# A transformer block in one hand-ordered kernel: down weights on SP's queue, and the order dealt anew

## The chip, the cores and the metric

The kernel runs on one core of a Trainium2 chip. A core has five engines with a queue of instructions each: TensorE (PE in the profile; its weight loads are listed as PEld), VectorE (DVE), ScalarE (ACT), GpSimd (POOL) and SyncE (SP), which here only issues transfers. Each takes its instructions in order and waits at semaphores. Transfers are carried by 16 DMA engines that all queues share. The metric is the time of one execution on the device in microseconds (us); the time before is the median of three runs.

## The reference

Input is x with 2048 rows of 1024, in bf16. Attention has 32 heads of 32 for the queries and one head for keys and values; the second half is a gated block with 3584 hidden columns.

```
h  = x + attention(layernorm(x)) @ wo
     q = layernorm(x) @ wq   (32 heads),  k, v = layernorm(x) @ wk, @ wv   (one head)
     p = softmax(q k^T / sqrt(32)),  o = p v
h2 = h + (sigmoid(n @ w_gate) * (n @ w_up)) @ w_down      with n = layernorm(h)
```

## The kernel before, in words

The 2048 rows are 16 tiles of 128; two tiles are a *unit*, so there are eight units. Keys and values of all rows and the queries are made first, then attention and the gated block run interleaved: while one unit is in attention, earlier ones are in the gated block.

**Attention** is cut into 512 *bursts*. A burst is four score matmuls side by side (line 888), which fill two pairs of PSUM banks, and two exponentials of 128 x 1024 on ScalarE (line 908) that read them into bf16 tiles (`Pr`, at first also free parts of `QT` and `wo`). There are three pairs of banks, so burst k waits for the first exponential of burst k-1. The products with V follow in chains of eight steps (line 995), with VectorE adding up the exponentials for the sums (945, 957) and matmuls with ones finishing them (1042, 1057).

**The rest of TensorE's work** goes between bursts, in *steps* of one 512-column matmul (line 382) or of four 32-column matmuls side by side (line 384) that do the same work; eight steps accumulate into one of two PSUM banks. Such groups are the output projection of a tile, gate or up columns of a tile (256 x 2 columns each), and the down projection (28 steps). A gate group is evacuated by ScalarE (tanh, line 1359), an up group by VectorE (1399), which writes `gu`; SP transposes that to `hact` (1383). After the output projection VectorE takes the second layernorm's statistics; GpSimd makes mean and reciprocal deviation (473 to 488), VectorE writes `hn`, and SP transposes it into `QT` (line 633): only then can gate and up of this tile begin.

**Weights.** Gate and up weights come again for every unit in *slabs* of 512 KB (`load_halves`), into whichever buffer is free: `wgu`, used-up parts of `QT`, at the end `Pr`, `kT4` and `zone`. If only a unit's first tile is ready, a slab may be held for the second tile (`may_hold`) or is loaded once more. The down weights stay: 14 loads of 512 KB into `zone` (`load_wd`), as the room of the queries' weights and of the transposed first layernorm comes free.

**What sets the order.** The Python that builds the program keeps a clock for each engine and one for the transfers (`k_dma`). Each instruction adds a written cost to its engine's clock, each transfer or transposition gets a time at which it counts as landed (`dma`, `transposed`), and the main loop chooses what TensorE does next by what counts as ready: the next burst when the exponential it waits for counts as done (`due`), otherwise attention chains by the letters of `PV_PLAN`, or a group. `PV_HOLD` says how long past that moment a chain may go on. Where a long stretch has nothing ready, `fill` puts in matmuls of 128 columns that nobody reads (line 418). So the order is fixed in the program; on the chip the semaphores alone decide when each instruction starts, and a transfer that lands later than it was counted stops the engine at that place, with everything behind it.

In `load_wd` GpSimd waits for the matmuls that last read the room, and for the last 12 loads also for an exponential, so that the load isn't issued early:

```
                need(pool, *ticks)
                if wd_next[0] >= NFP - WD_LATE:
                    need(pool, (c_e, 2 * k[0] - 2))
```

`LN_LEAD` and `LN_RATE` say how many tiles of the first layernorm must be done before some query work, `T_PLAN` and `Q_PLAN` which engine evacuates query tiles, `TODO` the order of the first groups, `U_PLAN` when a unit's output projection is urgent, `TURN` when down loads pause ahead of a transposition, `I_MAX` how many instructions of column-tiled steps may be dense.

Of the kernel before, what the change touches and what calls it, by code (L numbers as in the profile page):

```python
# [12 lines left out]
P = 128  # L13
# [73 lines left out]
def bass_sequential_preLN__grouped_kv_mqa__glu_gated_glu__prompt_kernel(  # L87
# [23 lines left out]
    NFP = NFT // 2  # L111
# [5 lines left out]
    RP = 18  # L117
    HR = 4
    NGU = 4
    U_PLAN = "07293057"  # L120
    PV_PLAN = "EAaabCdaAbadaDdbDAbaCeBDadaadaaaAaaaaAaaDbaBaaaaaadaBBDaaabCaaEdAbDaABDA"
    WO_PLAN = "bbbaabba"
    PV_HOLD = 1.25
    BANK_WAIT = 0
    NPB = 4
    G_SUM, HCH, HB0 = 4, 4, 2
    LN_LEAD = 3
    LN_RATE = 0.25
    T_PLAN = "aaaaddaddaddddad"
    H_ROOM = 0.2  # L130
    Q_PLAN = "ddaaadddddddaddddddddddddddddddd"
    SUM_PLAN = "ppppdddp"
    HOLD0 = 2
    HOLD7 = 2
    D_PLAN = "00000000"
    K_BUSY = 10
    TODO = ["q1b", "q3c", "C1", "q3b", "q1a", "v0", "Q4", "q0d", "q3a", "k1", "k2", "q2b", "C3", "q2a", "v4", "v6",
            "k3", "q1d", "C2", "v3", "v7", "v5", "q1c", "q0c", "v1", "q2c", "q2d", "q3d", "v2"]
# [14 lines left out]
    NU = len(UNITS)  # L153
    UNIT = {t_: c_ for c_, ts_ in enumerate(UNITS) for t_ in ts_}
    LAST_G = [max(g_ for g_, x_ in enumerate(ORDER) if UNIT[x_[0]] == c_) for c_ in range(NU)]
    WD_FROM, WD_GAP, WD_LATE = 10, 3, 12
    WD_GAP2 = 1
    TURN = 0
    LATE = 0.05
    I_BLOCK, I_LAT = 256, 4.5  # L160
    H_GAP = 3
# [1 line left out]
    H_LEAD = 2.0  # L163
    H_OUT = 4
    QREC = 32
    QORD = 0
    URG0 = 0
    K_ACT = 0
    T_MM, T_FIX, T_SW, T_EXP, T_TANH, T_ADD = 0.0004167, 0.00267, 0.0985, 0.9165, 0.479, 0.61

    xf = A_x[0]
# [2 lines left out]
    with ExitStack() as es:  # L174
# [33 lines left out]
        k_pe, k_dve, k_act, k_pool, k_sp, k_dma = [0.0], [0.0], [0.0], [0.0], [0.0], [0.0]  # L208
# [13 lines left out]
        d_wo, d_wd = ctr("d_wo"), ctr("d_wd")  # L222
# [55 lines left out]
        def _(unused):  # L278
            sp, pe, act, dve, pool = nc.sync, nc.tensor, nc.scalar, nc.vector, nc.gpsimd

            def dma(q, dst, src, c, kb=256, rate=285.0, lat=None):
                q.dma_start(dst, src).then_inc(c.sem, 16)
                c.n += 16
                begin = max(CLK[id(q)][0], k_dma[0])
                k_dma[0] = begin + kb / rate
                c.at[c.n] = k_dma[0] + (lat or 1.15 + kb * 0.0037) + (0.8 if q is pool else 0.0)
                return (c, c.n)

# [69 lines left out]
                need(pe, f(True) if callable(f) else f)  # L358
                bank_free[b] = "open"

            main = [False]

            issued = collections.deque()
            part = [0]
            I_US, I_MAX = 4.0, 210

            def by_columns(g):
                if not main[0] or g.items[0][0] < 0.05:
# [261 lines left out]
            def transposed(eng, dst, src, slot, *ticks):  # L630
                need(eng, *ticks)
                c, clk = d_t[slot], CLK[id(eng)]
                eng.dma_start_transpose(dst, src).then_inc(c.sem, 16)
                c.n += 16
                queued = eng is sp and len(x_val) == NT and k_dma[0] > clk[0]
                clk[0] += 1.3
                if eng is sp:
                    k_dma[0] = max(clk[0], k_dma[0]) + 1.2
                c.at[c.n] = max(clk[0], k_dma[0] if eng is sp else 0.0) + (1.9 if queued else 0.7)
                return (c, c.n)  # L640

            k_val, v_val, q_val = {}, {}, {}
# [1063 lines left out]
            def turning():  # L1706
# [175 lines left out]
```

## Time and profile before

| | us |
|---|---|
| median of three runs (1089.45 to 1093.27) | 1090.58 |
| profiled execution | 1090.78 |
| its span | 1089.0 |
| TensorE busy | 1055.4 |
| ScalarE busy | 1008.4 |
| VectorE busy | 900.1 |
| GpSimd busy | 64.5 |

Busy times are of the span. A matmul of 512 columns is listed with some 380 ns, but the next one starts long before its end, so busy TensorE isn't TensorE at its peak; the exponentials on ScalarE overlap in the same way. In the rows by time a bracket such as [0.45 <-PE S_ps L888] is idle time of the engine before the row, and what ended it. In the rows on waits stand the total, the number and the longest. The chain goes back from the last instruction to what released each step; a DMA row in it runs from issue to landing.

### The profile page before, as it was taken

The page shows a single profiled execution, that of the slowest core. Times are in us where ns is not written, and L with a number is a line of the kernel's source. Part 1 is how long each engine was busy: PE and PEld are TensorE (multiplying, and loading weights), DVE is VectorE, ACT ScalarE, POOL GpSimd, SP SyncE. Part 2 cuts the span into 40 slices and gives each one's busy share as a digit, 9 for nine tenths or more (in the row PEclk, how much of TensorE's full clock was granted, in tenths as well). Part 3 has the DMA queues.
Part 4 walks back from the last instruction along what each step waited for, and adds up shares of the span by engine and source line. Part 5 has one row for each costly group of instructions (what it writes and reads, how often), then busy time and mean ns, then how long its engine had stood idle before and what let it go on. Part 6 is the DMA issues. An engine that isn't in the chain of part 4 may idle for free.

```text
span 1089.0 us, 25646 instructions
## 1 busy us (share of the span) xinstructions
PE 1055.4 (97%) x10436; PEld 424.9 (39%) x10537; DVE 900.1 (83%) x1491; ACT 1008.4 (93%) x1152; POOL 64.5 (6%) x136
## 2 busy tenths in 40 slices
PE   8999999999999999999999999999999999999999
PEld 7643333333333333333333333333333333333344
DVE  6889888888988888899988897889888989879621
ACT  6999999999999999999999999999999999999410
POOL 2341111000000000000000000000000000000000
PEclk9999999999999999999999999999999999999999
DMA  7557359953989469982999649990999459990880
GB/s 195 123 120 234 88 129 267 213 122 112 299 203 282 117 160 268 259 196 79 291 247 248 177 106 303 242 250 27 269 296 304 121 152 292 309 298 21 233 236 25
DMA packets 278677, 215.46 MB, mean 198 GB/s; under 512 B 100256, under 2 KB 272544, under 8 KB 278560
## 3 DMA queue, kind: packets, MB, share of 16 engines
q1 hardware_dynamic: 273744, 204.12, 72.5%
q0 software_dynamic: 2592, 9.44, 3.1%
q8 instruction: 83, 1.36, 0.5%
q10 hardware_dynamic: 2224, 0.26, 0.2%
q14 instruction: 34, 0.28, 0.1%
HBM read 187.30 MB, written 4.19 MB: 176 GB/s over the span
## 4 chain that ended last, share of the span: by engine, by line
PE 79%; ACT 8%; DMA 6%; issue 4%; DVE 3%; POOL 1%; SPq 0%; POOLq 0%; ACTq 0%
PE X_ps L382 44%; PE X_ps L384 13%; PE S_ps L888 13%; PE X_ps L995 9%; ACT Pr L908 7%; DMA wgu<-in_B_w_up_dram 2%; DMA QT<-hn 1%; DMA wgu<-in_B_w_gate_dram 1%; DMA zone<-in_A_wv_dram 1%; ACT wo L908 1%; DMA QT<-in_B_w_up_dram 1%; PE X_ps L1042 1%; DVE pairs L945 1%; POOL sd L484 0%; PE X_ps L1057 0%
## 5 line engine op out<-in xcount | busy, mean ns | idle before, releaser
L908 ACT ACTIVATE Pr<-S_ps 128x1024 bf16<-128x1024 f32 x992 | 933.8, 1066 | 6.7 <-PE S_ps L888 6.0
L945 DVE TENSOR_TENSOR pairs<-Pr 128x1024 bf16<-128x1024 bf16 x470 | 320.6, 684 | 30.5 <-ACT Pr L908 29.7
L957 DVE TENSOR_TENSOR pairs<-pairs 128x1024 bf16<-128x1024 bf16 x408 | 281.6, 690 | 12.1
L888 PE MATMUL S_ps<-QT,kT 32*128 32x512 bf16 x2048 | 202.0, 385 | 4.7 <-ACT wo L908 1.1
L382 PE MATMUL X_ps<-wgu,QT 128*128 128x512 bf16 x777 | 198.0, 380 | 7.2 <-issue 3.7
L382 PE MATMUL X_ps<-zone,hact 128*128 128x512 bf16 (+2 forms) x675 | 156.4, 371 | 4.0 <-issue 3.5
L888 PEld LDWEIGHTS S_ps<-QT,kT 32*128 32x128 bf16 x2048 | 51.5, 91 | 211.3 <-ACT Pr L908 198.1
L382 PE MATMUL X_ps<-QT 128*128 128x512 bf16 x480 | 124.0, 380 | 5.2 <-issue 2.2
L995 PE MATMUL X_ps<-Pr,V 128*32 128x512 bf16 x1984 | 126.9, 381 | 0.6 <-ACT Pr L908 0.6
L1399 DVE SCALAR_TENSOR_TENSOR gu<-gu,X_ps 128x512 bf16<-128x512 f32 x112 | 76.6, 684 | 44.8 <-PE X_ps L382 38.1
L382 PEld LDWEIGHTS X_ps<-wgu,QT 128*128 128x128 bf16 x817 | 71.5, 98 | 99.2 <-issue 22.2
L1359 ACT ACTIVATE gu<-X_ps 128x512 f32<-128x512 f32 x112 | 71.3, 636 | 36.2 <-PE X_ps L382 36.2
L382 PEld LDWEIGHTS X_ps<-zone,hact 128*128 128x128 bf16 x705 | 60.9, 98 | 78.2 <-issue 19.3
L995 PEld LDWEIGHTS X_ps<-Pr,V 128*32 128x32 bf16 x1984 | 46.6, 96 | 57.1 <-issue 14.1
L382 PEld LDWEIGHTS X_ps<-QT 128*128 128x128 bf16 x504 | 44.3, 98 | 61.6 <-issue 12.7
L382 PE MATMUL X_ps<-wo,QT 128*128 128x512 bf16 x232 | 58.1, 380 | 0.9 <-issue 0.5
L473 POOL CAST mean<-mv 128x1 f32<-128x1 bf16 x28 | 6.6, 235 | 864.3 <-DVE mv L1210 832.4
L384 PE MATMUL X_ps<-zone,hact 128*32 128x512 bf16 x876 | 55.4, 380 | 0.0
L382 PE MATMUL X_ps<-zone 128*128 128x128 bf16 (+3 forms) x548 | 49.5, 238 | 2.5 <-DVE QT L772 0.8
L384 PE MATMUL X_ps<-wgu,QT 128*32 128x512 bf16 x748 | 51.1, 381 | 0.4 <-DVE ols L1087 0.2
L384 PE MATMUL X_ps<-QT 128*32 128x512 bf16 x688 | 46.4, 380 | 1.3 <-DVE olp L1011 0.6
L1435 DVE SCALAR_TENSOR_TENSOR hx<-X_ps,hx 128x512 bf16<-128x512 f32 (+2 forms) x33 | 22.2, 672 | 24.4 <-PE X_ps L382 22.6
(116 smaller groups left out, 612.8 us busy)
## 6 DMA issues: line engine op xcount, KB each, us to landing
wgu<-in_B_w_up_dram SPq DMA_DIRECT2D x90, 512.0 KB, 6.1
wgu<-in_B_w_gate_dram SPq DMA_DIRECT2D x87, 512.0 KB, 6.0
QT<-in_B_w_gate_dram SPq DMA_DIRECT2D x65, 512.0 KB, 6.3
QT<-in_B_w_up_dram SPq DMA_DIRECT2D x64, 512.0 KB, 6.2
zone<-in_B_w_down_dram POOLq DMA_DIRECT2D x14, 512.0 KB, 4.8
hx<-in_A_x_dram SPq DMA_DIRECT2D x17, 256.0 KB, 2.8
out_dram<-hx SPq DMA_DIRECT2D x31, 128.0 KB, 1.7
Pr<-in_B_w_gate_dram SPq DMA_DIRECT2D x5, 512.0 KB, 6.4
```

The lines of the kernel that those rows point to most:

```text
L382: return pe.matmul(out, lhsT=lhsT, rhs=rhs, start=start, stop=stop, skip_group_check=main[0])
L384: ins = pe.matmul(out[DH * j:DH * (j + 1)], lhsT=lhsT[:, DH * j:DH * (j + 1)], rhs=rhs, start=start, stop=stop, tile_position=(0, DH * j), ...
L473: return c_pool.inc(pool.tensor_copy(out=mean[:, i:i + 1], in_=mv[:, i:i + 1, 0]), 0.2)
L888: ins = pe.matmul(S_ps[:, ((2 * k + j // 2) % 3) * 2 + j % 2, :], lhsT=kT4[DH * j:DH * (j + 1), kt * P:(kt + 1) * P], rhs=rows(t)[DH * j:D ...
L908: c_e.inc(act.activation(out=p_tile(k, n % 2), in_=S_ps[:, 2 * pr:2 * pr + 2, :].rearrange("p a (b q) -> p (a b) q", q=QC), func=ACTF.Exp, ...
L945: slot_use[x] = c_dve.inc(dve.tensor_tensor(out=dst(x), in0=p_tile(k - 1, hh), in1=p_tile(k, hh), op=ALU.add), T_ADD, 0.08)
L957: slot_use[x] = slot_use[y] = c_dve.inc(dve.tensor_tensor(out=pairs[:, x, :], in0=pairs[:, x, :], in1=pairs[:, y, :], op=ALU.add), T_ADD, ...
L995: ins = pe.matmul(bank[DH * j:DH * (j + 1), :], lhsT=V[:, kt, :], rhs=p_tile(kx, j // 2)[:, j % 2 * 2:j % 2 * 2 + 2, :], start=b == bs[0], ...
L1042: ins = pe.matmul(bank[DH * j:DH * (j + 1), :], lhsT=ones[:], rhs=pairs[:, sum_wide[(g, j // 2)], j % 2 * 512:(j % 2 + 1) * 512], start=Tr ...
L1359: tanh_val[n] = c_act.inc(act.activation(out=slot, in_=bank, func=ACTF.Tanh, scale=0.5), T_TANH, 0.1)
L1399: v = c_dve.inc(dve.scalar_tensor_tensor(out=slot.bitcast(BF16)[:, 0:512], in0=slot, scalar=1.0, in1=bank, op0=ALU.add, op1=ALU.mult), 0.6 ...
L1435: v = c_dve.inc(dve.scalar_tensor_tensor(out=hv, in0=bank[:, 0:n], scalar=0.5, in1=hv, op0=ALU.mult, op1=ALU.add), 0.03 + n * 0.00113, 0.08)
```

## The change

The 14 loads of down weights go to SP's queue, where the slabs and the transpositions are issued, and are counted there as slabs are; GpSimd's waits for exponentials fall away, and with them the use of `WD_LATE`. A transposition that is queued behind other transfers counts as landing 3.1 us after its turn instead of 1.9, another one in the main loop 1.5 instead of 0.7. GpSimd's remaining transfers count as slower. `PV_HOLD` falls from 1.25 to 0.5, `BANK_WAIT` and the other numbers change as shown, and with new costs and plans the order of the whole program is dealt anew. No work of the reference is added or removed; the number of gate and up slabs falls from 320 to 304, the fillers of line 418 rise from 89 to 154.

```
-    U_PLAN = "07293057"
+    U_PLAN = "75761920"
...
-    PV_HOLD = 1.25
-    BANK_WAIT = 0
+    PV_HOLD = 0.5
+    BANK_WAIT = 0.3
...
-    LN_LEAD = 3
-    LN_RATE = 0.25
-    T_PLAN = "aaaaddaddaddddad"
+    LN_LEAD = 1
+    LN_RATE = 0.35
+    T_PLAN = "aaaaaddddddaadaa"
...
-    WD_FROM, WD_GAP, WD_LATE = 10, 3, 12
+    WD_FROM, WD_GAP, WD_LATE = 10, 3, 14
     WD_GAP2 = 1
-    TURN = 0
+    TURN = 1
...
-    QORD = 0
-    URG0 = 0
-    K_ACT = 0
+    QORD = 1
+    URG0 = 1
+    K_ACT = 1
...
                 begin = max(CLK[id(q)][0], k_dma[0])
-                k_dma[0] = begin + kb / rate
+                k_dma[0] = begin + kb / (200.0 if q is pool else rate)
...
-            I_US, I_MAX = 4.0, 210
+            I_US, I_MAX = 4.0, 180
...
-                c.at[c.n] = max(clk[0], k_dma[0] if eng is sp else 0.0) + (1.9 if queued else 0.7)
+                c.at[c.n] = max(clk[0], k_dma[0] if eng is sp else 0.0) + (3.1 if queued else 1.5 if main[0] else 0.7)
...
                 i, ticks = wd_free.popleft()
-                need(pool, *ticks)
-                if wd_next[0] >= NFP - WD_LATE:
-                    need(pool, (c_e, 2 * k[0] - 2))
+                need(sp, *ticks)
                 wd_next[0] += 1
                 wd_at[0] = k[0] + (WD_GAP if not q_list else WD_GAP2)
-                wd_val[0] = dma(pool, wd[:, 2 * i:2 * i + 2, :],
-                                B_w_down[2 * i * P:2 * (i + 1) * P, :].rearrange("(a p) n -> p a n", p=P), d_wd, 512)
+                wd_val[0] = dma(sp, wd[:, 2 * i:2 * i + 2, :],
+                                B_w_down[2 * i * P:2 * (i + 1) * P, :].rearrange("(a p) n -> p a n", p=P), d_wd, 512, 340.0, 2.9)
+                k_sp[0] += 0.45
```

Two lines that end up elsewhere in the file make the line numbers after the change one or two higher (888 becomes 889, 633 becomes 634, 282 becomes 284).

**On SP, around the second tile's transposition.** `QT<-hn` is the transposition of a normalized tile, `hact<-gu` that of a gated block, `wgu<-in_B_w_gate_dram` and the like are slabs, `zone<-in_B_w_down_dram` is a down load. Before:

```order
L633 DMA_TRANSPOSE QT<-hn 128x8x128
L282 DMA hx<-in_A_x_dram 128x1024 x2
L1383 DMA_TRANSPOSE hact<-gu 128x4x128
L633 DMA_TRANSPOSE QT<-hn 128x8x128
L1383 DMA_TRANSPOSE hact<-gu 128x4x128
L282 DMA wgu<-in_B_w_gate_dram 128x4x512 x2
L282 DMA wgu<-in_B_w_up_dram 128x4x512
L1383 DMA_TRANSPOSE hact<-gu 128x4x128
```

And after:

```order
L634 DMA_TRANSPOSE QT<-hn 128x8x128
L284 DMA hx<-in_A_x_dram 128x1024
L284 DMA zone<-in_B_w_down_dram 128x2x1024 x2
L284 DMA hx<-in_A_x_dram 128x1024
L1384 DMA_TRANSPOSE hact<-gu 128x4x128
L634 DMA_TRANSPOSE QT<-hn 128x8x128
L1384 DMA_TRANSPOSE hact<-gu 128x4x128
L284 DMA zone<-in_B_w_down_dram 128x2x1024
L284 DMA wgu<-in_B_w_gate_dram 128x4x512
L284 DMA zone<-in_B_w_down_dram 128x2x1024
L284 DMA wgu<-in_B_w_gate_dram 128x4x512
L1384 DMA_TRANSPOSE hact<-gu 128x4x128
```

Down loads now stand between the slabs. Up to the third tile's transposition it is seven of them and 22 slabs on SP; before it was 24 slabs there, and six down loads in the same stretch on GpSimd.

**On TensorE, where the second tile's gate begins.** `X_ps<-zone,QT` is a gate or up step on a slab in `zone`, `X_ps<-Pr,V` a product with V, `S_ps<-QT,kT` a burst. Before (burst 72 is the first row):

```order
L888 MATMUL S_ps<-QT,kT 128x512 x4
L995 MATMUL X_ps<-Pr,V 32x512 x28
L888 MATMUL S_ps<-QT,kT 128x512 x4
L995 MATMUL X_ps<-Pr,V 32x512 x4
L384 MATMUL X_ps<-zone,QT 32x512 x20
L888 MATMUL S_ps<-QT,kT 128x512 x4
```

And after, from burst 73 on:

```order
L889 MATMUL S_ps<-QT,kT 128x512 x4
L996 MATMUL X_ps<-Pr,V 32x512 x24
L889 MATMUL S_ps<-QT,kT 128x512 x4
L419 MATMUL X_ps<-kT 128x128 x19
L383 MATMUL X_ps<-zone,QT 128x512
L889 MATMUL S_ps<-QT,kT 128x512 x4
```

The second tile's first steps stood behind the last product with V, five of them ahead of the next burst; now 19 fillers and one step stand between two bursts. Over the whole program, past burst 24, the stretches between two bursts that have nine steps are 64 before and 71 after; one has ten and one eleven before, none after.

**On TensorE, behind the last burst.** `X_ps<-wo,QT` is the last tile's output projection, `S_ps<-hn` its transposition on TensorE; the other 512-column rows are gate and up steps. Before:

```order
L384 MATMUL X_ps<-QT 32x512 x8
L995 MATMUL X_ps<-Pr,V 32x512 x4
L384 MATMUL X_ps<-QT 32x512 x16
L995 MATMUL X_ps<-Pr,V 32x512 x4
L1042 MATMUL X_ps<-pairs,ones 32x512 x4
L1057 MATMUL X_ps<-Pr,ones 32x512 x8
L382 MATMUL X_ps<-QT 128x512 x4
L382 MATMUL X_ps<-kT,QT 128x512 x4
L382 MATMUL X_ps<-wo,QT 128x512 x16
L382 MATMUL X_ps<-QT 128x512 x8
L382 MATMUL X_ps<-Pr,QT 128x512 x8
L1252 MATMUL S_ps<-hn 128x128 x8
```

And after:

```order
L996 MATMUL X_ps<-Pr,V 32x512 x28
L385 MATMUL X_ps<-wgu,QT 32x512 x12
L996 MATMUL X_ps<-Pr,V 32x512 x4
L1043 MATMUL X_ps<-pairs,ones 32x512 x4
L1058 MATMUL X_ps<-Pr,ones 32x512 x8
L383 MATMUL X_ps<-QT 128x512 x8
L383 MATMUL X_ps<-wgu,QT 128x512 x4
L383 MATMUL X_ps<-QT 128x512 x4
L383 MATMUL X_ps<-wo,QT 128x512 x16
L383 MATMUL X_ps<-QT 128x512 x4
L383 MATMUL X_ps<-kT,QT 128x512 x4
L383 MATMUL X_ps<-Pr,QT 128x512 x11
```

Sixteen steps instead of eight stand between the last sums and the output projection, 19 instead of 16 between it and the transposition (which follows the last row here). Counted to the end of the program, behind the last burst stand 276 matmuls of 512 columns and 44 column-tiled ones before, 300 and 56 after. On ScalarE, 11 gate activations stood behind the last exponential, and now 13.

More of the change, by code (lines that the diff above doesn't have):

```diff
@@ L119, in bass_sequential_preLN__grouped_kv_mqa__glu_gated_glu__prompt_kernel @@
     NGU = 4
-    U_PLAN = "07293057"
-    PV_PLAN = "EAaabCdaAbadaDdbDAbaCeBDadaadaaaAaaaaAaaDbaBaaaaaadaBBDaaabCaaEdAbDaABDA"
-    WO_PLAN = "bbbaabba"
-    PV_HOLD = 1.25
-    BANK_WAIT = 0
+    U_PLAN = "75761920"
+    PV_PLAN = "aDAcebaAAaaEaAaaAaBdCadabcbEaaaaaCEaAAAaaAEAbaacbbaAaAadabbaEAabbDacabab"
+    WO_PLAN = "abaabbbb"
+    PV_HOLD = 0.5
+    BANK_WAIT = 0.3
     NPB = 4
     G_SUM, HCH, HB0 = 4, 4, 2
-    LN_LEAD = 3
-    LN_RATE = 0.25
-    T_PLAN = "aaaaddaddaddddad"
+    LN_LEAD = 1
+    LN_RATE = 0.35
+    T_PLAN = "aaaaaddddddaadaa"
     H_ROOM = 0.2
-    Q_PLAN = "ddaaadddddddaddddddddddddddddddd"
+    Q_PLAN = "ddaadddddddddddddddddddddddddddd"
     SUM_PLAN = "ppppdddp"
@@ L136, in bass_sequential_preLN__grouped_kv_mqa__glu_gated_glu__prompt_kernel @@
     K_BUSY = 10
-    TODO = ["q1b", "q3c", "C1", "q3b", "q1a", "v0", "Q4", "q0d", "q3a", "k1", "k2", "q2b", "C3", "q2a", "v4", "v6",
-            "k3", "q1d", "C2", "v3", "v7", "v5", "q1c", "q0c", "v1", "q2c", "q2d", "q3d", "v2"]
+    TODO = ["q1a", "q1b", "v0", "C3", "q3c", "q3b", "C1", "q2a", "k3", "q2b", "q3a", "Q4", "q0d", "k1", "v7", "v4",
+            "C2", "k2", "q1d", "v1", "v6", "q2d", "q1c", "v2", "v5", "q3d", "q0c", "q2c", "v3"]
     ORDER = [(0, 0), (1, 0), (0, 2), (1, 2), (0, 1), (0, 3), (1, 1), (1, 3)]
@@ L279, in _ @@
             sp, pe, act, dve, pool = nc.sync, nc.tensor, nc.scalar, nc.vector, nc.gpsimd
+            main = [False]
             def dma(q, dst, src, c, kb=256, rate=285.0, lat=None):
@@ L359, in open_group @@
                 bank_free[b] = "open"
-            main = [False]
             issued = collections.deque()
             part = [0]
-            I_US, I_MAX = 4.0, 210
+            I_US, I_MAX = 4.0, 180
             def by_columns(g):
```

## The prediction, made blind

> **What bounds the kernel now.** I read the head of the page first, then the waits, then ScalarE and TensorE in order of time where they wait, and the chain.
>
> ```profile
> span 1089.0 us, 25646 instructions
> PE 1055.4 (97%) x10436; PEld 424.9 (39%) x10537; DVE 900.1 (83%) x1491; ACT 1008.4 (93%) x1152; POOL 64.5 (6%) x136
> ACT  6999999999999999999999999999999999999410
> ```
>
> ScalarE is full from the second slice to the 37th, TensorE everywhere. There are two stages: until about 1018 us ScalarE's exponentials go on, and behind them TensorE works alone.
>
> ```profile
> PEld S_ps L888 <- ACT Pr L908: 198.1, 467, 0.7
> ACT Pr L908 <- PE S_ps L888: 6.0, 9, 1.3
> POOL mean L473 <- DVE mv L1210: 832.4, 16, 76.5
> POOL zone L282 <- ACT Pr L908: 64.6, 10, 21.8
> ```
>
> The first row decides the first stage: 467 of the 512 score bursts waited for an exponential, so there ScalarE sets the pace and TensorE fits its other work in between. ScalarE itself shows only 6.0 us of waiting for a burst. These are the long ones, in ScalarE's order of time:
>
> ```profile
> 133.92 1.94 ACT L908 ACTIVATE Pr<-S_ps 128x1024 bf16<-128x1024 f32 x2 [0.25 <-PE S_ps L888]
> 136.30 2.86 ACT L908 ACTIVATE Pr<-S_ps 128x1024 bf16<-128x1024 f32 x3 [0.45 <-PE S_ps L888]
> 139.03 0.62 ACT L1359 ACTIVATE gu<-X_ps 128x512 f32<-128x512 f32 x1
> 139.51 8.45 ACT L908 ACTIVATE Pr<-S_ps 128x1024 bf16<-128x1024 f32 x9
> ...
> 155.27 1.02 ACT L908 ACTIVATE Pr<-S_ps 128x1024 bf16<-128x1024 f32 x1 [1.32 <-PE S_ps L888]
> ...
> 176.62 1.94 ACT L908 ACTIVATE Pr<-S_ps 128x1024 bf16<-128x1024 f32 x2 [0.78 <-PE S_ps L888]
> ...
> 196.41 3.77 ACT L908 ACTIVATE Pr<-S_ps 128x1024 bf16<-128x1024 f32 x4 [1.05 <-PE S_ps L888]
> ...
> 665.83 1.02 ACT L908 ACTIVATE Pr<-S_ps 128x1024 bf16<-128x1024 f32 x1 [1.09 <-PE S_ps L888]
> ...
> 958.32 1.94 ACT L908 ACTIVATE Pr<-S_ps 128x1024 bf16<-128x1024 f32 x2 [0.56 <-PE S_ps L888]
> ```
>
> Two prices come from here. A gate activation pushes the next exponential back by 0.48 us (139.03 to 139.51). Nine exponentials take 8.45 us and one alone 1.02, so one follows the other after (8.45 - 1.02)/8 = 0.93; they overlap by about 0.1, so an idle shown costs 0.1 more than it says. The chain and TensorE's rows tell what made those four bursts late that show 0.78 and more:
>
> ```profile
> 149.18 4.43 DMA QT<-hn
> 166.82 10.32 DMA wgu<-in_B_w_gate_dram
> 187.90 7.06 DMA wgu<-in_B_w_up_dram
> 655.37 8.38 DMA QT<-hn
> ...
> 1016.12 1.99 ACT Pr L908 x2
> ```
>
> The last row is the end of the exponentials: 1018.1 us. TensorE's rows at the first of those places:
>
> ```profile
> 151.70 0.40 PE L995 MATMUL X_ps<-Pr,V 128*32 128x512 bf16 x4
> 153.65 1.26 PE L384 MATMUL X_ps<-zone,QT 128*32 128x512 bf16 x20 [1.55 <-DMA QT<-hn]
> 154.84 0.39 PE L888 MATMUL S_ps<-QT,kT 32*128 32x512 bf16 x4
> ```
>
> Two are transpositions of a normalized tile that landed later than the order had assumed, two are slabs of gate or up weights. In each case TensorE stood before a step, and the next burst stood behind it. The other three idles come from long stretches of attention work between two bursts: at 136.30 nine column-tiled steps (a step is one 512-wide matmul, or four column-tiled ones side by side), at 958.32 ten.
>
> **The second stage** is pure TensorE work:
>
> ```profile
> 1041.16 10.74 PE X_ps L382 x49
> ...
> 1051.95 10.74 PE X_ps L382 x49
> ```
>
> From 1041.16 to 1051.95 are 49 steps: 0.22 us a step. Whatever is not done when the last burst is issued costs this price in full. TensorE's waits there, from 1015 us on:
>
> ```profile
> PE X_ps L995 <- ACT Pr L908: 0.6, 1, 0.6
> PE X_ps L382 <- DVE QT L1103: 0.4, 1, 0.4
> PE X_ps L382 <- DVE olp L1015: 0.4, 1, 0.4
> PE S_ps L1252 <- DVE hn L492: 0.4, 1, 0.4
> ```
>
> The profiled execution took 1090.78 us, 1.8 more than its span, 0.2 above the median of 1090.58 shown. I work out the difference on the span and add it to the median.
>
> **The change, part by part.**
>
> *Work left for the end: +5.9.* Behind the last score burst stand 276 full steps and 44 column-tiled matmuls (11 steps) before, 300 and 56 (14) after; the narrow ones at the very end are the same. That is 27 steps more, 27 x 0.22 = 5.9 us. The kernel's whole work is the same, so three groups of eight steps, with some attention work, have moved from the first stage, where ScalarE's pace hides them, to the second, where nothing does. This term is surest: it holds for any time at which the last burst comes.
>
> *ScalarE's own work in the first stage: -1.0.* As many exponentials as before stand there; but 99 gate activations before the last of them instead of 101, 2 x 0.48. Its evacuations of projected tiles stay nine, of the same size. Ends: -0.5 (one of the two already hidden in a wait) and -1.0.
>
> *Late data in the first stage: -3.8.* The four idles above are 1.32 + 0.78 + 1.05 + 1.09 = 4.2, with 0.1 each for the overlap 4.6. At the first place five steps stood between the wait of 1.55 and the next burst. Now 19 fillers stand ahead of the wait, 1.3 us at 6.3/89 each (row below), and one step behind it, so a transposition as late as before makes TensorE wait about 0.3 us with a short stretch to take it up: no late burst. At 665 us I expect the same, since a queued transposition is now counted 1.2 us later. With slabs it is less clear. The new order loads 304 of them instead of 320 (held slabs serve both tiles in four more cases), but between the second and the third tile's transposition, where the two late slabs were, it is 22 slabs and seven down loads against 24 and six. How full the DMA engines were:
>
> ```profile
> core 0: us, PE busy (x) PEld busy (x) DVE busy (x) ACT busy (x) POOL busy (x), PEclk, DMA share, GB/s
> 140.00:200.00 60.00, 54.81 (x421) 20.36 (x427) 48.78 (x78) 56.72 (x66) 6.04 (x9) 1.00 0.86 205
> 200.00:650.00 450.00, 440.35 (x4190) 165.02 (x4233) 395.15 (x633) 449.53 (x511) 11.82 (x24) 1.00 0.77 199
> 650.00:670.00 20.00, 18.26 (x153) 6.95 (x156) 17.76 (x30) 18.86 (x23) 1.77 (x3) 1.00 0.98 239
> ```
>
> Both troubled stretches have the fullest DMA engines, so fewer transfers help. Bounds: -4.6 if all four waits go, +4.4 if none does and two new ones come (the slower rival). I take -3.8, nearest to the first end: the two transpositions (2.4, with overlap 2.6) gone by the order at the first place, and 1.2 of the slabs' 2.0, since the fillers moved there too (18 together ahead of burst 80, where 7 stood).
>
> *Long stretches: -1.2.* The idles at 133.92, 136.30 and 958.32 are 1.26, with overlap 1.6. Past the start, two stretches between bursts have ten or more steps before, none after; but 71 instead of 64 have nine, so a quarter is left. Ends: 0 and -1.6.
>
> *Waits in the end stage: -1.2.* The four rows sum to 1.8. Sixteen steps (3.5 us) instead of eight now stand between the last sums and the output projection, more than the 1.7 us of the present eight plus the 0.4 that was missing; nineteen instead of sixteen (0.66 more) cover the last transposition, against 0.4; and three steps more stand before the last attention step, 0.66 against 0.6. The wait for the bank (0.4) stays. Ends: 0 and -1.8.
>
> *At nothing:* the 65 more filler matmuls, which stand where TensorE would wait for ScalarE anyway (without that cover, 89 of them take 6.3 us by the row below, so 65 some 4.6). The 14 loads' issue on SP, 0.53 us as in the row below: SP waits between its transfers (its longest sum of waits is below too), so only what stands just behind is later by that much; uncovered, all 14 cost 7. GpSimd loses 14 issues and their 64.6 us of waiting for exponentials, but the row above shows that all its 16 statistics casts waited for VectorE, none for a down load: no gain.
>
> ```profile
> L418 PE MATMUL X_ps<-kT 128*128 128x128 bf16 x89 | 6.3, 219 | 0.0
> ```
>
> ```profile
> 175.77 0.53 SPq L282 DMA_DIRECT2D wgu<-in_B_w_up_dram  x1
> ```
>
> ```profile
> SPq L282 <- DVE hx L1435: 198.2, 31, 10.4
> ```
>
> ```profile
> zone<-in_B_w_down_dram POOLq DMA_DIRECT2D x14, 512.0 KB, 4.8
> ...
> wgu<-in_B_w_gate_dram SPq DMA_DIRECT2D x87, 512.0 KB, 6.0
> ```
>
> Sum: 5.9 - 1.0 - 3.8 - 1.2 - 1.2 = -1.3 us.
>
> **Rivals.** *Slabs late behind the down loads (slower).* A down load lands 4.8 us after its issue from GpSimd, a slab 6.0 from SP, though both are 512 KB: from its own queue the down load gets in between. In line it goes ahead of every slab issued later. At 205 GB/s with a share of 0.86, full engines move 238 GB/s, so 512 KB take 2.2 us, and a slab just behind is late by up to that. Seven down loads stand there. If none of the four old waits goes, the sum is 5.9 - 1.0 - 1.2 - 1.2 = +2.5; with two new slab waits of 2.2 it is +6.9. From my sum it takes 4.6 us, two full ones, to pass the 3.3 us (0.3%) that a measurement of this kernel can tell from no change. For it: the slabs of this stretch were already late twice. Against it: 29 transfers fall into it instead of 30, and the order counts a down load's place in the line.
>
> [...]
>
> *Nearly all waits go (faster by over 0.3%).* At their far ends the terms are 5.9 - 1.0 - 4.6 - 1.6 - 1.8 = -3.1; and ScalarE's 6.0 us of waits shown hold 1.8 outside the four, of which the long stretches took 1.3, so -3.6; short waits below a burst's overlap of 0.1, over 512 bursts, may add one or two, so some -4.5. For it: 16 slabs less and later-counted transpositions everywhere. Against it: it needs every term.
>
> *The waits only move.* The order avoids the old places, and as many late transfers turn up at others: +2.5 without new losses. Against it is the first place, where filler now stands in for the wait.
>
> **How the numbers follow.** My forecast has 0.48: 1090.6 - 1.3 = 1089.3 us, its own range 1086.8 to 1092. Nearly all waits go: 0.26, about 1086. Slabs late: 0.19, 1093 to 1098. Waits only move: 0.07, about 1093. Over 0.3% faster is below 1087.3: 0.10 of the forecast and 0.24 of the second case, 0.34. Over 0.3% slower is above 1093.9: 0.19 of the third and 0.04 of the fourth, 0.23. The rest, 0.43, is within 0.3%. The range of 8 in 10 goes from 1085.3 (past the second case) to 1094.3 (past the fourth, into the third).
>
> **What would show it.** Right: the last exponential ends about 6 us earlier than 1018.1 (1.0 + 3.8 + 1.2), and from there to the end is about 4.7 us longer (5.9 - 1.2); ScalarE's waits for bursts fall from 6.0 to about 2; no transposition of a normalized tile holds TensorE by over a microsecond at 150 and 660 us. Wrong: a slab (wgu or QT from w_gate or w_up) in the chain with 8 us or more between 140 and 230 us; or an end stage that is not 27 steps longer; or a last exponential at the old time.

## The result

Timed in turn on one chip, eight runs of each, the changed kernel takes 1086.55 us in the median (1086.17 to 1088.25) and the kernel before 1092.68 (1089.45 to 1094.49). The ratio is 0.9949, with a 95% interval of 0.9935 to 0.9963: 0.5% faster. The profiled executions are 1086.67 us with a span of 1084.9, against 1090.78 and 1089.0, so 4.1 us lie between the two traces, against 5.6 by the ratio. The kernel before varies more from run to run than the changed one, and where the granted clock of TensorE is on record for its executions, its longer ones are mostly those with a clock below 1.00 (last section); both traces have 1.00, so what follows accounts for the 4.1.

The head of the page after:

```profile
span 1084.9 us, 25541 instructions
PE 1057.7 (97%) x10408; PEld 430.0 (40%) x10509; DVE 898.8 (83%) x1491; ACT 1006.0 (93%) x1152; POOL 54.7 (5%) x122
ACT  6999999999999999999999999999999999999310
```

The bound is the same: ScalarE is full until shortly before the end. The turn from the first stage to the second is what moved. ScalarE's last exponentials stand in this row of its timeline (start, duration, then how many in a row):

```profile
1004.78 4.79 ACT L909 ACTIVATE Pr<-S_ps 128x1024 bf16<-128x1024 f32 x5
```

They end at 1009.57, against 1018.11 before: 8.5 us earlier. From there to the end of the span it is 75.3 us against 70.9: 4.4 longer. The difference is the 4.1 us.

Where the first stage lost its time is seen in ScalarE's idle time by stretches, each cut at the same times, up to the last exponential. Before:

```profile
0.00:22.00 22.00, 17.76 (x257) 15.10 (x257) 14.70 (x43) 11.96 (x18) 4.72 (x14) 1.00 0.83 210
...
130.00:230.00 100.00, 94.19 (x785) 35.27 (x795) 83.12 (x135) 95.90 (x111) 10.10 (x18) 1.00 0.82 192
230.00:640.00 410.00, 401.59 (x3850) 150.65 (x3895) 359.48 (x575) 409.65 (x465) 9.98 (x20) 1.00 0.77 199
640.00:680.00 40.00, 37.49 (x381) 13.98 (x377) 33.75 (x54) 38.86 (x46) 1.77 (x3) 1.00 0.99 262
...
sum 1018.11, PE 988.08 PEld 393.15 DVE 882.01 ACT 1001.22 POOL 63.21; mean PE 164.68 PEld 65.53 DVE 147.00 ACT 166.87 POOL 10.53
```

And after (the columns are length, then busy time and instructions of PE, PEld, DVE, ACT and POOL, then granted clock, DMA share and GB/s):

```profile
0.00:22.00 22.00, 19.56 (x287) 17.12 (x288) 15.74 (x45) 12.89 (x21) 4.81 (x15) 1.00 0.89 223
...
130.00:230.00 100.00, 96.82 (x870) 37.44 (x878) 86.06 (x140) 99.21 (x115) 3.16 (x7) 1.00 0.81 207
230.00:640.00 410.00, 401.56 (x3807) 151.80 (x3847) 358.65 (x573) 408.09 (x464) 10.78 (x21) 1.00 0.75 195
640.00:680.00 40.00, 39.23 (x350) 15.41 (x352) 36.65 (x60) 40.00 (x48) 1.67 (x3) 1.00 1.01 265
...
sum 1009.57, PE 985.36 PEld 395.60 DVE 879.63 ACT 997.59 POOL 53.38; mean PE 164.23 PEld 65.93 DVE 146.61 ACT 166.27 POOL 8.90
```

From 130 to 230 us ScalarE stood idle for 4.1 us before and 0.8 after, from 640 to 680 for 1.1 and none: the two stretches with the late transpositions and slabs. In the long stretch between them it is idle 1.6 us more than before (0.35 to 1.91). In all, up to the last exponential, the idle time falls from 16.9 to 12.0, by 4.9; the busy time falls by 3.6.

ScalarE's waits for score bursts, the bursts' weight loads' waits for exponentials, and the two transfers left in the chain that ended last, after:

```profile
ACT Pr L909 <- PE S_ps L889: 1.4, 3, 0.8
PEld S_ps L889 <- ACT Pr L909: 201.2, 475, 1.1
```

```profile
187.00 6.75 DMA wgu<-in_B_w_up_dram
...
280.64 6.17 DMA wgu<-in_B_w_gate_dram
```

ScalarE's waits fell from 6.0 us in nine to 1.4 in three. No transposition of a normalized tile is in the chain, and TensorE's waits in the first stage show none for one. The DMA queues after (issues, KB each, median us from issue to landing):

```profile
wgu<-in_B_w_up_dram SPq DMA_DIRECT2D x86, 512.0 KB, 5.6
wgu<-in_B_w_gate_dram SPq DMA_DIRECT2D x86, 512.0 KB, 5.5
...
zone<-in_B_w_down_dram SPq DMA_DIRECT2D x14, 512.0 KB, 5.9
```

A down load lands 1.1 us later than from GpSimd (4.8 before), a slab half a microsecond earlier (6.0 and 6.1 before).

In the end stage TensorE's blocks run as before, 49 steps in 10.74 us, and its waits from 1007 us on are two instead of four:

```profile
PE X_ps L1043 <- ACT gu L1360: 0.5, 1, 0.5
PE X_ps L383 <- issue: 0.2, 1, 0.2
```

### The profile page after: what moved, and what is told of

It reads as the page before. It is cut to its first block, busy times and chain, and to the rows that moved or that the text cites. A ratio compares the mean times of both kernels' runs of the same rounds, so it can differ in the third digit from the quotient of the medians.

```text
span 1084.9 us, 25541 instructions
## 1 busy us (share of the span) xinstructions
PE 1057.7 (97%) x10408; PEld 430.0 (40%) x10509; DVE 898.8 (83%) x1491; ACT 1006.0 (93%) x1152; POOL 54.7 (5%) x122
## 4 chain that ended last, share of the span: by engine, by line
PE 81%; ACT 8%; DVE 6%; issue 3%; DMA 1%; POOL 0%; ACTq 0%
PE X_ps L383 46%; PE S_ps L889 13%; PE X_ps L385 12%; PE X_ps L996 9%; ACT Pr L909 5%; DVE pairs L946 2%; DVE pairs L958 2%; ACT wo L909 1%; ACT QT L909 1%; PE X_ps L1043 1%; PE X_ps L1058 1%; DMA wgu<-in_B_w_up_dram 1%; DMA wgu<-in_B_w_gate_dram 1%; PE X_ps L564 1%; DVE gu L1400 0%
## 5 line engine op out<-in xcount | busy, mean ns | idle before, releaser
L383 PE MATMUL X_ps<-zone,hact 128*128 128x512 bf16 (+2 forms) x685 | 159.2, 371 | 3.7 <-issue 3.5
L383 PE MATMUL X_ps<-QT 128*128 128x512 bf16 x477 | 121.1, 380 | 2.9 <-issue 2.4
L383 PE MATMUL X_ps<-zone 128*128 128x128 bf16 (+3 forms) x572 | 52.8, 240 | 1.5 <-ACT zone L591 0.4
L385 PE MATMUL X_ps<-zone,hact 128*32 128x512 bf16 x836 | 52.6, 380 | 0.2 <-DVE ols L1088 0.2
L385 PE MATMUL X_ps<-QT 128*32 128x512 bf16 x656 | 43.8, 380 | 0.4 <-DVE gu L1400 0.4
```

The costliest lines, as they stand in the source:

```text
L383: return pe.matmul(out, lhsT=lhsT, rhs=rhs, start=start, stop=stop, skip_group_check=main[0])
L385: ins = pe.matmul(out[DH * j:DH * (j + 1)], lhsT=lhsT[:, DH * j:DH * (j + 1)], rhs=rhs, start=start, stop=stop, tile_position=(0, DH * j), ...
```

## The experiments

The question was which part of the change carries the gain: the other queue, the later-counted transpositions, or the new order as such; and whether late data was the cause at all. In the first six kernels below, the order of the instructions on TensorE, ScalarE and VectorE is, row for row, that of the kernel they start from.

**The queue alone, in the order before.** The 14 down loads are issued by SP, at the places in the program at which GpSimd had them, without the wait for exponentials (`by` names the engine that issues; the planner's own counting is left as it was):

```diff
-                    need(pool, (c_e, 2 * k[0] - 2))
...
+                for t in ticks:
+                    t[0].wait(sp, t[1])
...
-                                B_w_down[2 * i * P:2 * (i + 1) * P, :].rearrange("(a p) n -> p a n", p=P), d_wd, 512)
+                                B_w_down[2 * i * P:2 * (i + 1) * P, :].rearrange("(a p) n -> p a n", p=P), d_wd, 512, by=sp)
```

> The kernel before with its order kept to the row; only the 14 down loads are issued by SP, at the same places in the program, without the wait for exponentials. Theory (order): within 1 us of the kernel before, ratio 1.000, the idles of ScalarE at about 155 and 666 us unchanged. Rival (queue): the two waits for slabs, 0.8 and 1.1 us of ScalarE's idle time, go; ratio 0.998.

Measured: 1090.52 us, ratio to the kernel before 0.9984 (0.9965 to 1.0003). ScalarE's waits hardly fall, and the transposition near 150 us still makes a burst late by more than a microsecond:

```profile
ACT Pr L908 <- PE S_ps L888: 5.6, 11, 1.2
```

```profile
154.48 1.02 ACT L908 ACTIVATE Pr<-S_ps 128x1024 bf16<-128x1024 f32 x1 [1.19 <-PE S_ps L888]
```

The two bursts that slabs had made late near 176 and 196 us no longer wait by more than 0.16 us, as the rival had it, but waits of 0.44 to 0.58 turn up at four other places, two of them right behind a slab (187.72 and 272.26). So the queue by itself gives no gain that these runs can tell from none.

**The order alone, the down loads back on GpSimd.** The changed kernel, with its 14 down loads issued by GpSimd, without waits for exponentials:

```diff
-                need(sp, *ticks)
+                for t in ticks:
+                    t[0].wait(pool, t[1])
...
+                                pool)
```

> The changed kernel's order on TensorE, VectorE and ScalarE kept to the row; only the 14 down loads are issued by GpSimd again. If the gain sits in the order (my theory), this stays within 1 us of the changed kernel, ratio to the kernel before about 0.995. If the queue itself matters (rival: from GpSimd's queue a down load takes turns with the slabs and makes them late), it loses 1.5 to 3 us of the gain, ratio 0.996 to 0.998, with new waits for slabs between 150 and 200 us.

Measured: 1095.75 us, ratio 1.0027 (1.0007 to 1.0046): what the new order gains is lost without the queue, and by the two ratios the kernel is 8.5 us slower than the changed one. That is beyond both forecasts. By the times of the bursts' weight loads it is 0.5 us behind the changed kernel at burst 56, 2.3 at burst 72 and 10 at burst 88; the last exponential ends at 1018.1, 8.5 later. The chain names what was late, and GpSimd's timeline what was ahead of it:

```profile
130.59 7.62 DMA QT<-hn
151.35 7.79 DMA QT<-hn
168.87 13.25 DMA wgu<-in_B_w_up_dram
```

```profile
129.93 1.49 POOL L284 DMA_DIRECT2D zone<-in_B_w_down_dram  x2
150.70 2.21 POOL L284 DMA_DIRECT2D zone<-in_B_w_down_dram  x3
```

Two and three down loads, 1 and 1.5 MB, are issued within 2.2 us around the transposition that TensorE needs next. The two land in 7.6 and 7.8 us, where the one at 149.18 took 4.43 before. In the changed kernel the same two take 3.0 and 3.3 us: SP issues the second at 149.06 and the next down load at 151.68, behind it. Nothing on GpSimd holds a load to its place in SP's order.

**The same, with the loads held near their places.** Each load now also waits on GpSimd for the exponential two bursts behind its place in the order, as the late ones did before the change:

```diff
+                if 2 * k[0] - 2 <= c_e.n:
+                    c_e.wait(pool, 2 * k[0] - 2)
```

> The changed kernel's order, its 14 down loads issued by GpSimd as in the run without waits, but each load now waits on GpSimd for the exponential two bursts behind the place at which the order puts it. In the run without waits three down loads were issued one right after the other and the slabs and transpositions beside them landed in 7.6 to 13 us, 9.2 us of ScalarE waiting. Theory 'bunching': it is the early, bunched issue that costs, not the queue; with the loads spread to their places the time is that of the changed kernel, 1086.5 to 1088.5, and ScalarE waits 3 us or less for score bursts. Rival 'the queue': down loads on another queue than the slabs' get in between them wherever they are issued; then at least half of the 8.6 us stays, 1091 or more, ScalarE's waits 5 us or more, and a slab in the chain with 8 us or more between 130 and 200 us.

Measured: 1091.02 us, ratio 0.9995 (0.9980 to 1.0011). ScalarE waits 4.3 us for score bursts, a little below the bound that the rival gave, and the slab of 8 us or more is there:

```profile
181.32 10.69 DMA wgu<-in_B_w_gate_dram
```

```profile
177.13 1.44 POOL L284 DMA_DIRECT2D zone<-in_B_w_down_dram  x2 [5.76 <-PE X_ps L383]
```

The transpositions are in time again: SP issues them at 130.80 and 149.78, GpSimd the loads behind them only at 135.49 and 153.16, and TensorE's waits show none over 0.6 us for a transposition of a normalized tile. But two down loads issued together at 177 us stand before slabs that are issued at 180. So both theories hold in part: of the 8.5 us, 3.5 go with the bunching at 130 and 151 us, and 5.0 (by the ratios) stay. These 5.0 are not shown to be the queue's alone. SP issues the same two loads at 176.81 and 180.54 in the changed kernel, the second behind two gate slabs, so even here one load runs ahead of the order; a run that puts each load exactly at SP's place was not made.

**Is it contention with slabs?** The order and queue of the run without waits, with half of each slab of gate and up weights left out (except those held in the large buffer, `zone`), so that the gated block is computed with wrong weights:

```diff
-    half_val[u] = dma(sp, halves[i]..., src, d_sl[i], 512, ...)
+    nl = 4 if i > H_KT else 2
+    half_val[u] = dma(sp, halves[i]...[:, 0:nl, :], src[:, 0:nl, :], d_sl[i], 512, ...)
```

> The changed kernel's order with both earlier edits: half of each slab of gate and up weights not loaded (except those held in the large buffer), so that the gated block is computed with wrong weights, and the 14 down loads issued by GpSimd without waits. On whole slabs the down loads on GpSimd cost 8 to 9 us, on half slabs in line the changed kernel took 1085.7. Theory 'contention': the loads on GpSimd cost because they take the DMA engines from slabs and transpositions that are needed at once; with half slabs nothing is late any more, 1085 to 1088, ScalarE's waits for score bursts below 2 us. Rival 'GpSimd itself': what costs is what stands behind the 14 issues on GpSimd, the statistics' casts and the normalized tiles that wait for them; then half slabs do not help and the time is 1092 to 1095.

Measured: 1094.55 us, ratio 1.0023 (1.0003 to 1.0042). The theory of contention with slabs missed. No slab is late any more, but the two transpositions still are:

```profile
130.66 8.63 DMA QT<-hn
152.43 7.46 DMA QT<-hn
```

ScalarE's waits are 8.8 us, all but 0.2 of them in five rows between 141 and 170. The rival's condition came true as a time, but not by its mechanism: the transpositions are issued at nearly the same time as in the run before (130.66 against 130.59, 152.43 against 151.35) and are late between issue and landing. Against the changed kernel (130.09 and 149.06) the second is issued 3.4 us later, behind bursts that were late already, so what stands behind GpSimd's issues can have only a part in it. What is left is the down loads in flight beside a transposition. In the changed kernel, with the loads in line on SP, the two transpositions take 3.0 and 3.3 us. With the same half slabs and the loads in line (the changed kernel with half slabs, below) TensorE's waits show none over 0.4 us for them, and in the run with held loads, where no load is issued just ahead of them, none over 0.6. Down loads are not the only thing that can do this: the transposition at 655.37 in the kernel before took 8.38 us, long after the last down load, and with half slabs it no longer made TensorE wait. The transposition's bytes were not changed in any run, so whether it is its share of the DMA engines or its place behind their packets is not settled.

**Is the gain late data at all?** The same half slabs, in the kernel before and in the changed one (the gated block again with wrong weights):

> The kernel before, order kept to the row, but every slab that doesn't go into zone loads only half of its rows (the other half of its buffer is left as it was, so the gated block is computed with wrong weights). If the four late bursts are late data, as predicted, ScalarE's four idles go and the last exponential ends 4 to 5 us earlier than 1018.1; ratio 0.995 to 0.996. If those waits are not the transfers' (rival), under 2 us are won. If more transfers were late than ScalarE shows, over 6 us are won.

> The changed kernel with half slabs in the same way (the gated block is computed with wrong weights). It has two idles of ScalarE at slabs left (195 and 288 us, 1.6 us by start to start), so the theory gives 1 to 2 us below the changed kernel, ratio 0.993 to 0.994. If the new order had only moved the late data about (rival), 4 us or more are won here too, ratio 0.991 or less.

Measured: 1085.36 us for the order before (ratio 0.9930, 0.9899 to 0.9961) and 1085.67 for the new one (0.9929, 0.9900 to 0.9958). With half slabs the two orders take the same time, as far as these runs can tell. In the order before the last burst comes 5.0 us earlier than with whole slabs, in the new one 1.4, both as expected. In the order before, TensorE's wait for the transposition near 150 us stays (first row). The steps that waited 1.02 us for the one issued at 655 us with whole slabs now start without a wait (second row):

```profile
153.44 1.26 PE L384 MATMUL X_ps<-zone,QT 128*32 128x512 bf16 x20 [1.60 <-DMA QT<-hn]
...
659.10 1.04 PE L382 MATMUL X_ps<-QT 128*128 128x512 bf16 x4
```

So late data is what the gain over the kernel before rests on: where none is late behind a slab, the longer end stage of the new order (75.4 us, against 70.9) is just paid by its shorter first stage. That stage is still 4.9 us shorter with half slabs (its last exponential ends at 1008.2 against 1013.1), where it was 8.5 with whole ones. So 3.6 of the 8.5 go with the size of the slabs; the wait of 1.60 above is in the other 4.9, and the rest of these was not taken apart.

**The fillers.** The changed kernel without its 154 filler matmuls (10.5 us of TensorE), all else in its order:

```diff
-                for i in range(n):
-                    pe.matmul(X_ps[:, free[0], 0:P], lhsT=kT4[:, 0:P], ...)
```

> The changed kernel without its 154 filler matmuls (10.5 us of TensorE), all else in the same order. The prediction had the 65 more fillers at nothing. By that the time is within 1 us of the changed kernel's, 1085.5 to 1087.6, with a share of TensorE's waits for exponentials that is larger by about 10 us and the same waits of ScalarE. Rival 'they cost': they stand ahead of steps at moments when TensorE was not waiting for ScalarE; then without them the last exponential ends 1 to 3 us earlier, 1083.5 to 1085.5. Rival 'they keep something up': without them a granted clock below 1.00 in the profile and matmuls longer than now, and a longer time by several us.

Measured: 1086.35 us, ratio 0.9957 (0.9940 to 0.9974): as with them. TensorE now waits where they stood, and ScalarE does not:

```profile
PEld S_ps L886 <- ACT Pr L906: 202.2, 468, 1.6
...
PE S_ps L886 <- ACT Pr L906: 9.6, 14, 1.5
...
ACT Pr L906 <- PE S_ps L886: 0.6, 2, 0.4
```

The fillers cost nothing that shows in the median, and they bring nothing there either. One sign of the last rival is on record: four of the ten executions without fillers have a granted clock of 0.997 or 0.998 and take 1087.43 to 1090.40 us, the six others 1.00 and 1085.73 to 1086.46; all eight of the changed kernel have 1.00. These are too few to show that fillers keep the clock up. In the trace without them (clock 1.00) the transposition near 150 us makes TensorE wait 0.8 us, and no burst is late there: with one step behind the wait, no filler is needed ahead of it.

**The counting alone.** The kernel before with its own table of numbers, but with the down loads on SP, the later transpositions and GpSimd's slower transfers counted, and the order dealt anew by that; then the changed kernel with the transpositions counted as before, also dealt anew:

```diff
-                c.at[c.n] = max(clk[0], k_dma[0] if eng is sp else 0.0) + (1.9 if queued else 0.7)
+                c.at[c.n] = max(clk[0], k_dma[0] if eng is sp else 0.0) + (3.1 if queued else 1.5 if main[0] else 0.7)
```

> The other half of the change alone: the kernel before with its own table of numbers, but the down loads on SP and the later transpositions counted, dealt anew by these. Behind the last score burst stand 347 steps against 314 in the changed kernel and 287 before. Theory 'the order avoids late data because these are counted': the transpositions no longer hold TensorE by over a microsecond and ScalarE waits 1 us or less for bursts, so the last exponential comes 5 to 9 us earlier than before; the end is 60 steps longer, 60 x 0.22 = 13.2 us, so the time is 1095 to 1099, slower than before. Rival 'the table avoids them': with the old table the waits of ScalarE stay at 4 us or more, and the time is 1099 or more. Rival 'the counting is all of the gain and the end adapts': 1086 to 1088.

Measured: 1099.53 us, ratio 1.0076 (1.0050 to 1.0102). From the last exponential to the end it is 82.7 us, 11.8 longer than before (60 steps, 13.2 expected), and the last exponential comes only 2.9 earlier. ScalarE's waits did not fall, and a transposition counted later still holds TensorE:

```profile
ACT Pr L908 <- PE S_ps L888: 6.9, 8, 2.1
```

```profile
156.11 0.61 PE L382 MATMUL X_ps<-zone,QT 128*128 128x512 bf16 x2 [1.36 <-DMA QT<-hn]
```

That is the rival: the new counting by itself does not take the waits away, the table has to go with it.

> The changed kernel with one thing undone: a transposition counted as landing after 1.9 and 0.7 us as before, not 3.1 and 1.5, and the order dealt anew by that. 339 steps stand behind the last score burst, 25 more than in the changed kernel: 25 x 0.22 = 5.5 us in the end stage. Theory 'the counted latency is what takes the transpositions' waits away': one or more transpositions hold TensorE by over a microsecond again and ScalarE waits 3 us or more for bursts, so the first stage gains little from the work it sheds; 1091 to 1095. Rival 'the latency counted does not matter, the dealing does': ScalarE's waits stay below 1.5 us, the first stage sheds most of the 25 steps' time only where ScalarE does not set the pace, so 1089 to 1092 with the whole loss in the end stage.

Measured: 1102.23 us, ratio 1.0096 (1.0064 to 1.0128), slower than either theory gave. The end is 81.3 us, 6.0 longer than in the changed kernel (5.5 expected). Transpositions hold TensorE again, by up to 1.1 us, but ScalarE waits only 2.4 us for score bursts. Most of what the first stage lost (its last exponential comes 8.9 us later) stands in neither forecast: the new dealing put a long row of projections between two early bursts.

```profile
24.43 5.18 PE L383 MATMUL X_ps<-zone 128*128 128x128 bf16 x94 [0.39 <-DVE kT L677]
29.55 0.40 PE L889 MATMUL S_ps<-QT,kT 32*128 32x512 bf16 x4
```

```profile
22.00:60.00 38.00, 35.64 (x629) 24.53 (x626) 32.53 (x76) 33.25 (x40) 15.05 (x35) 1.00 0.66 117
```

ScalarE is idle for 4.8 us of these 38, where the changed kernel's has none. So this run does not price the latency by itself: any number changed deals the whole order anew, and what that costs (here some 6 us at the start) is larger than what was to be measured. What the counted latency alone is worth stays open.

## Why the prediction was right, and where it was off

The sign of the forecast was right, and so was its way of working: a longer end, a shorter first stage, the first stage's gain larger. Its own number, 1089.3, was 2.8 us above the time measured, which lies just below the forecast's own range (from 1086.8); the case that came is the second rival, nearly all waits go, about 1086. The change in the traces, -4.1 us against -1.3 forecast, is off by the same 2.8, nearly all of it in the first stage.

- *Work left for the end, +5.9*, and *waits in the end stage, -1.2*: right. The sum was 4.7 and 4.4 was measured. The waits fell from 1.8 us to 0.7, by 1.1, so the added steps cost 5.5.
- *ScalarE's own work, -1.0*: not contradicted. As many gate activations as counted stand before the last exponential, and each still pushes the next one back by 0.48 us (the median over 99). ScalarE's busy time fell by 3.6 us. Beside the 1.0 and the overlap of 0.1 lost at each idle, some two microseconds lie in the start and in many intervals between exponentials, too little in each to be seen; they are not assigned.
- *Late data, -3.8*, and *long stretches, -1.2*: right in kind and nearly in size. One row was read wrongly: the slab at 166.82 with 10.32 us lands at 177.14, after the burst at 176.62 that it is said to have held. TensorE's wait there, 0.77 us, ended at 175.67, by the gate slab issued just ahead on SP (165.96); so it was a slab, but another one. Past the start, ScalarE's idle time fell by 4.0 us as shown (6.9 to 2.9: 4.4 less in the two stretches, and 0.4 more elsewhere); with 0.1 for each of the six waits for bursts that went, some 4.6 of the 5.0. With the term before, the forecast for the last exponential was 6.0 us earlier, and it came 8.5 earlier. Of the 2.5 between, about 1.4 was there by burst 24, ahead of the down loads; the unchanged order with its loads on SP showed 0.9 of the same kind there, and two more runs of the new order's start 0.6 and 0.9, so half of it or more is how one execution differs from another. The remaining 1.1 lie in the part of the busy time that is not assigned; they may be the short delays that the second rival named and the sum left out. So the 2.5 that the forecast missed in the first stage is not assigned. That the gain rests on late data is shown by the half slabs: with them the orders are equal.
- *At nothing: the queue and GpSimd.* This is the step that failed. The prediction gave the move of the 14 loads no gain, since no statistics cast waited for one, and saw in it only a risk for slabs behind. In the order before it is indeed worth nothing that shows (ratio 0.9984). But the new order depends on it: with the loads on GpSimd it is 5.0 us slower when they are held near their places and 8.5 when they are not, and the last exponential falls back to 1018.1 in the latter. The term of -3.8 has as a condition that the loads are issued in line with the slabs, which the prediction did not say.
- *At nothing: the fillers.* Right, by the run without them. But the argument at the first place, that the filler takes up the wait, isn't needed there: without fillers and with one step instead of five behind the wait no burst is late.
- *The rival "slabs late behind the down loads"* did not come: no slab in the chain with 8 us or more from 140 to 230 us (6.75 at most), and slabs landing half a microsecond earlier in the median. It came where the loads were on GpSimd, at 168.87 with 13.25 and at 181.32 with 10.69. So slabs were late with the loads on the queue that was left. The two traces have the sign of that. Before, two down loads that GpSimd issued at 81.63 and 82.35 landed at 93.8 and 95.7, ahead of a gate slab that SP had issued at 80.75 (96.3); in the changed kernel all of SP's loads of weights and of x land in the order of their issue.
- *The signs to look for* came: the waits for bursts at 1.4 (about 2 forecast), no transposition that holds TensorE over a microsecond, 4.4 us more at the end (about 4.7).

## What to carry to other kernels

An order written for one queue is an order for that queue alone: price a queue and an order together, since here each half gave nothing measurable and both together 0.5%. Where a small transfer gates the engine that sets the pace, look at what other queues issue within the two microseconds around it; in these runs the loads on a queue that waited only for room ran ahead of the order, and a transposition beside them landed after 7.5 to 8.6 us, where it took 3.0 and 3.3 with the loads in line. And when a planner deals a whole program, undoing one of its numbers is no experiment on that number: keep the order fixed, row for row, and change the cost instead.

## What the runs showed of the hardware

**The granted clock of TensorE fell at late transfers in three runs.** In the trace of the changed kernel it is 1.00 throughout. With the loads on GpSimd, without waits, TensorE stood 4.14 us for the second transposition:

```profile
138.25 1.47 PE L383 MATMUL X_ps<-zone,QT 128*128 128x512 bf16 x6 [1.72 <-DMA QT<-hn]
...
159.20 0.61 PE L383 MATMUL X_ps<-zone,QT 128*128 128x512 bf16 x1 [4.14 <-DMA QT<-hn]
...
160.28 2.74 PE L383 MATMUL X_ps<-zone,QT 128*128 128x512 bf16 x6
```

```profile
156.00:160.00 4.00, 0.80 (x5) 0.21 (x5) 2.85 (x5) 0.01 (x1) 0.00 (x0) 0.62 0.97 201
160.00:164.00 4.00, 4.00 (x16) 1.07 (x13) 1.38 (x2) 2.33 (x3) 0.72 (x1) 0.52 0.27 76
164.00:168.00 4.00, 4.00 (x25) 1.43 (x23) 1.73 (x3) 3.87 (x5) 0.72 (x1) 1.00 0.73 254
```

For the four microseconds from 160 the clock is 0.52, six matmuls take 2.74 us that took 1.47 behind the first wait, and ScalarE, which the matmuls feed, is busy for 2.33; then the clock is back at 1.00. With half slabs and the loads on GpSimd the same happened at a wait of 3.80 us (159.94), and there a whole stretch shows 0.50:

```profile
136.00:140.00 4.00, 1.28 (x16) 0.42 (x9) 3.90 (x7) 2.58 (x3) 0.00 (x0) 1.00 0.50 154
...
156.00:160.00 4.00, 0.20 (x4) 0.07 (x1) 3.88 (x6) 1.09 (x2) 0.00 (x0) 0.86 1.14 261
160.00:164.00 4.00, 4.00 (x15) 0.99 (x15) 1.38 (x2) 1.94 (x2) 0.72 (x1) 0.50 0.28 71
164.00:168.00 4.00, 4.00 (x21) 1.42 (x18) 0.48 (x1) 3.46 (x5) 0.72 (x1) 0.79 0.83 192
```

If the clock was either 0.50 or 1.00, the means of the stretches give an estimate of how long it was low: (0.38 + 0.48) x 4 / 0.5 = 6.9 us in the first run and (0.14 + 0.50 + 0.21) x 4 / 0.5 = 6.8 in the second. By the same estimate it fell in the first run at 157.0 (0.38 x 4 / 0.5 = 3.0 us ahead of 160), which is 1.9 us into the wait and not at its end. So in these two runs a late transfer that held TensorE for some four microseconds cost more than the wait.

The run with held loads shows that the length of one wait isn't what counts: waits of 1.81 and 0.69 us with a burst and four matmuls between them were followed by a mean of 0.61; by the same estimate the clock was low for (0.03 + 0.39) x 4 / 0.5 = 3.4 us.

```profile
190.02 1.02 PE L383 MATMUL X_ps<-wgu,QT 128*128 128x512 bf16 x4 [1.81 <-DMA wgu<-in_B_w_gate_dram]
...
192.06 2.74 PE L383 MATMUL X_ps<-wgu,QT 128*128 128x512 bf16 x6 [0.69 <-DMA wgu<-in_B_w_gate_dram]
```

```profile
188.00:192.00 4.00, 1.56 (x9) 0.42 (x8) 3.38 (x6) 2.13 (x3) 0.72 (x1) 0.97 1.32 328
192.00:196.00 4.00, 3.94 (x14) 1.25 (x15) 0.00 (x0) 2.45 (x4) 0.00 (x0) 0.61 1.22 212
```

No fall followed the wait of 1.72 us above, nor one of 2.71 us with half slabs and the loads on GpSimd (it ended at 139.33; the clock is 1.00 from 128 to 156). TensorE's busy time in a stretch of four microseconds does not tell the cases apart either: from 188 to 192, where the fall began, it is 1.56 us, and from 136 to 140 with half slabs, without a fall, 1.28. What the clock goes by is not shown.

**A clock below 1.00 shows in the kernel before, too, from execution to execution.** In the three sets of runs that list the clock of its executions, 37 have 1.00 and take 1090.6 us in the median; the 17 others have 0.995 to 0.998 and take 1093.8. In the trace with held loads the 3.4 us of the estimate go with a mean of 0.998 over the execution. All eight executions of the changed kernel have 1.00. So the ratio of 0.9949 holds more than the 4.1 us of the traces, and the clock goes with the rest; what took the clock in those executions is in no trace.
